# First unit's q issued from ScalarE's queue, second unit's transposed q and k copied out in two parts, in a fused attention and two-layer kernel

## The chip, the cores and the metric

The kernel runs on one core of a Trainium2 chip. The metric is the device time of one execution in microseconds (us); of several runs the median is taken. The text calls the engines by the names of the profile: PE (matrix multiply) with its weight load PEld, DVE (vector), ACT (scalar, which also computes exp), POOL and SP. SP, ACT and POOL each have an instruction queue from which they issue DMA transfers; the rows of those issues carry the names SPq, ACTq and POOLq.

## The reference

Attention over 8 batches of 12 heads, 448 positions and head size 64, followed by two matrix products with a leaky ReLU between them:

```python
scores = (1 / sqrt(64)) * q @ k^T            # per batch and head: 448 x 448
attn = exp(scores - max) / (sum + 1e-9)
x = concat_heads(attn @ v)                    # 3584 x 768
h = x @ w_in                                  # 768 -> 2048
out = maximum(0.01 * h, h) @ w_out            # 2048 -> 768, float32
```

## The kernel before

One function builds the whole program, and the order of the instructions on each engine is written out by hand (a manual schedule; later stages are ordered by a small planner with a fixed model of times, which is evaluated while the program is built and so doesn't react to the run). The work is cut into 48 units: one unit is two heads of one batch. For each unit the kernel

1. loads q, k and v from HBM (`load_one`, line 170, as float32 on a given queue; `load_soft`, line 153, on POOL's queue with a cast to bfloat16 on the way);
2. rearranges or casts them to bfloat16 (`cast`, line 183: DVE for the first units, POOL later; for unit 0 the helper `both`, line 263, gives one head to ACT and the other to DVE);
3. turns q and k so that the head dimension lies on the partitions. For the first units PE does this (`transposes`, line 294): four transposes of 112 columns each for q and four for k, written into a PSUM bank and copied to the tile `qkT` (line 305). The two PSUM banks `g0` and `g1` are handed out alternately by `next_bank` (line 74);
4. computes score blocks: `scores(u, c)` (line 311), two matrix products per block, four blocks per unit, into three PSUM slots `sc` that go round;
5. applies exp on ACT to each block (`expo`, line 326; its operations have lines 331 and 334);
6. multiplies with v on PE (`pv`, line 365, whose products have line 362) and normalises on DVE (lines 374 and 375). The result is turned and becomes the input of `x @ w_in`.

The six units of the first batch are written out by `first(u)`. From unit 6 on, attention is interleaved with the matrix products of the two layers, which make up most of the program (lines 424, 548, 645, 682).

The start, around which the change lies, runs in this order. Lines 217 to 219 issue three loads on SP's queue: k of unit 0, q of unit 0, k of unit 1. Lines 222 to 229 issue, on POOL's queue, q of unit 1, q and k of units 2 and 3, v of unit 0 and so on. They all go to parts of the tile `w_in_mix`, and later to `w_mix`, which aren't needed for their own purpose yet. PE runs seven matrix products on a zeroed tile (`warm_up`, line 241). ACT loads its function table and makes a one-element copy (line 237). Then come the casts of unit 0, k first and then q, on ACT (line 264) and DVE (line 265) together.

`transposes(0)` is already in two parts, k and then q. After each part's four transposes stand five more products on the zeroed tile (`stay_warm`, line 247). k's part is copied out by ACT, q's part by DVE. `cast(1)` follows on DVE, q and then k. `first(0)` puts on PE the first three score blocks of unit 0, one more zeroed product, the eight transposes of unit 1 into one bank, and the fourth score block; DVE copies unit 1's turned q and k out of that bank in one operation of 128 x 896. `first(1)` continues with the scores of unit 1, which need both halves of that copy.

ACT, DVE and PE each work strictly in the order of the program. An instruction that waits holds up everything behind it on its engine.

Of the kernel before, what the change touches and what calls it, by code (L numbers as in the profile page):

```python
# [16 lines left out]
def kernel(  # L17
# [9 lines left out]
    nc = tc.nc  # L27
# [118 lines left out]
    def room(x, new):  # L146

        n = P if x and new else SC
        if not rooms:
            return ld_pool.tile([n, 2, NSC, D], F32, name="f" + "qkv"[x])  # L150
        return rooms.pop(0)[:n].bitcast(F32).rearrange("p (h so d) -> p h so d", h=2, so=NSC)
# [18 lines left out]
    def load_one(u, x, queue):  # L170
        b, hp = divmod(u, HP)
        t = room(x, False)
        queue.dma_start(
            out=t.rearrange("p h so d -> p h (so d)"),
            in_=(q, k, v)[x][b, 2 * hp:2 * hp + 2].rearrange("h (p so) d -> p h (so d)", so=NSC),
        )
        raw.setdefault(u, {})[x] = t
# [37 lines left out]
                nc.gpsimd.dma_start(out=o, in_=i)  # L215

    load_one(0, 1, nc.sync)
    load_one(0, 0, nc.sync)
    load_one(1, 1, nc.sync)
    ident = const_pool.tile([P, P], BF16)  # L220
    make_identity(nc, ident)
# [21 lines left out]
    def stay_warm(n):  # L243

        ps = next_slot()
        for _ in range(n):
            nc.tensor.matmul(ps[:, 0, :P], warm[:, :P], warm[:, :P], start=True, stop=True)
# [42 lines left out]
    def turn_tile(bank):  # L290
        bank = next_bank() if bank is None else bank
        return bank.bitcast(BF16)

    def transposes(u, bank=None):
        n = SC if u < HY else P
        t, flat = qkb[u % NB], qkT[u % NQ].rearrange("p i c s -> p (i c s)")[:, :2 * NSC * n]
        for parts in ((1,), (0,)) if u == 0 else ((0, 1),):
            tr = turn_tile(bank)[:, :2 * NSC * n].rearrange("p (i s) -> p i s", i=2)
            for i in parts:
                for so in range(NSC):  # L300
                    nc.tensor.transpose(tr[:, i, ts(so, n)], t[:n, i, so].rearrange("p h d -> p (h d)"), ident[:n, :n])  # L301
            if u == 0:
                stay_warm(5)
            at = slice(parts[0], parts[-1] + 1)
            (nc.scalar.copy if u == 0 and parts == (1,) else nc.vector.tensor_copy)(
                flat.rearrange("p (i s) -> p i s", i=2)[:, at], tr[:, at]
            )
# [301 lines left out]
    kept, parts = {}, []  # L609
# [257 lines left out]
    def first(u):  # L867
# [11 lines left out]
        if u == 1:  # L879
            transposes(u + 1)  # L880
# [5 lines left out]
        if u != 1:  # L886
            transposes(u + 1)
# [13 lines left out]


    transposes(0)
    cast(1, (0, 1), fast)
    for u in range(HP):
# [344 lines left out]
```

## Time and profile before

| what | value |
|---|---|
| median of three runs (lowest, highest) | 378.0 us (377.62, 378.05) |
| the profiled execution's own time | 377.8 us |
| its span in the profile | 376.0 us |
| busy: PE, DVE, ACT, POOL | 368.8, 255.9, 259.9, 190.6 us |
| first exp (ACT, line 331) starts | 6.36 us |
| DMA: bytes moved, mean rate | 48.08 MB, 128 GB/s |

The profile counts from the start of the span; the 1.8 us between the span and the execution's time lie outside it. A row of the timeline has the start, the duration, the engine, the line, the operation with its output and input tiles, and in brackets the time that the engine was idle before it and what ended that idle time. A row of DMA issues has the tiles, the queue, the number of issues, the size of each and the time from issue to landing. A row by windows has, for each stretch, the busy time and the number of instructions of each engine, the granted PE clock, the busy share of the 16 DMA engines and the rate.

### The profile page before, as it was taken

The numbers are of one execution on the slowest core, as the hardware profiler recorded it, in microseconds if no ns is written. First come the engines' busy times: TensorE is split into PE (matmuls) and PEld (weight loads), VectorE is DVE, ScalarE is ACT, GpSimd is POOL, SyncE is SP. The second block draws the span as 40 slices with busy tenths as digits, with TensorE's granted clock in tenths as the row PEclk, the third lists the DMA queues.
The fourth block names the chain that finished last, engine by engine and source line by source line (L and its number), as shares of the span: only waits on it lengthen the run. The fifth ranks groups of instructions, "written<-read, shape, count | busy, mean of one in ns | idle before, by whom it ended". The sixth has DMA issues, their size and how long they took to land.

```text
span 376.0 us, 10120 instructions
## 1 busy us (share of the span) xinstructions
PE 368.8 (98%) x4008; PEld 265.3 (71%) x4008; DVE 255.9 (68%) x559; ACT 259.9 (69%) x399; POOL 190.6 (51%) x376
## 2 busy tenths in 40 slices
PE   7999999999999999999999999999999999999996
PEld 3665658756698566996569966699665995679765
DVE  4764868767666967676686665875747775685763
ACT  6998895866768785758766587666787668636721
POOL 8985871996269979634588335692346020000000
PEclk9999999999999999999999999999999999999999
DMA  9999999999499876963969648999445740321123
GB/s 155 200 203 207 175 203 202 166 165 168 92 186 150 113 149 89 204 154 55 162 120 150 138 65 80 166 145 180 63 66 108 131 110 0 80 57 45 41 65 105
DMA packets 99600, 48.08 MB, mean 128 GB/s; under 512 B 64608, under 2 KB 96352, under 8 KB 99552
## 3 DMA queue, kind: packets, MB, share of 16 engines
q0 software_dynamic: 39600, 22.47, 45.6%
q1 hardware_dynamic: 59504, 24.50, 32.5%
q8 instruction: 31, 0.51, 0.6%
q10 hardware_dynamic: 448, 0.47, 0.4%
q14 instruction: 17, 0.14, 0.1%
HBM read 45.61 MB, written 11.01 MB: 151 GB/s over the span
## 4 chain that ended last, share of the span: by engine, by line
PE 95%; DMA 2%; DVE 1%; POOL 1%; ACT 1%; issue 0%; POOLq 0%; ACTq 0%
PE g L682 30%; PE g L548 14%; PE sc L548 14%; PE sc L322 7%; PE sc L350 6%; PE g L424 4%; PE sc L319 4%; PE sc L645 4%; PE sc L362 3%; PE g L820 2%; PE sc L343 2%; DMA w_in_mix<-in_v_dram 2%; PE g L362 1%; PE g L301 1%; PE sc L424 1%; POOL w_in_mix L163 1%
## 5 line engine op out<-in xcount | busy, mean ns | idle before, releaser
L331 ACT ACTIVATE e<-sc 128x896 bf16<-128x896 f32 (+1 forms) x144 | 123.6, 921 | 29.9 <-PE sc L322 20.4
L682 PE MATMUL g<-w_out_sb,h 128*128 128x384 bf16 (+1 forms) x440 | 84.1, 325 | 0.0
L682 PEld LDWEIGHTS <-h 128*128 128x128 bf16 x592 | 54.4, 98 | 41.2 <-issue 11.0
L537 ACT ACTIVATE h<-c 128x512 bf16<-128x512 f32 (+1 forms) x72 | 43.1, 610 | 30.2 <-DVE c L563 12.4
L548 PEld LDWEIGHTS <-w_in_sb 128*128 128x128 bf16 x576 | 54.6, 98 | 5.7
L190 POOL COPY qkb<-fq 112x512 bf16<-112x512 bf16 x34 | 22.6, 666 | 43.8 <-DMA qkT<-qkb 34.7
L548 PEld LDWEIGHTS <-w_in_mix 128*128 128x128 bf16 x432 | 40.5, 98 | 3.7
L201 POOL COPY v<-fv 128x384 bf16<-128x384 bf16 x30 | 17.7, 591 | 42.7 <-PE sc L350 40.2
L687 DVE COPY o<-g 128x384 f32<-128x384 f32 x47 | 26.0, 553 | 13.2 <-PE g L682 13.0
L350 PE MATMUL sc<-v,e 128*128 128x65 bf16 x720 | 33.3, 193 | 0.0
L322 PE MATMUL sc<-qkT 64*128 64x448 bf16 (+1 forms) x210 | 32.8, 352 | 0.0
L978 DVE RECIPROCAL rec<-sc 112x8 f32<-112x8 f32 x42 | 8.7, 207 | 34.7 <-PE sc L350 19.4
L350 PEld LDWEIGHTS <-e 128*128 128x128 bf16 x720 | 31.1, 98 | 1.3
L979 DVE TENSOR_TENSOR x<-sc,rec 112x512 bf16<-112x512 f32 x42 | 29.0, 691 | 1.6 <-DVE rec L978 0.2
L548 PE MATMUL g<-xT,w_in_sb 128*128 128x256 bf16 (+1 forms) x216 | 28.5, 268 | 0.0
L548 PE MATMUL sc<-xT,w_in_sb 128*128 128x256 bf16 (+1 forms) x216 | 28.5, 268 | 0.0
L693 DVE TENSOR_TENSOR o<-o,g 128x384 f32<-128x384 f32 x39 | 21.4, 550 | 9.0 <-PE g L682 4.4
L343 PE MATMUL sc<-v,e 128*128 128x130 bf16 x120 | 26.5, 221 | 0.0
L649 DVE TENSOR_TENSOR o<-o,sc 128x192 f32<-128x192 f32 x39 | 13.7, 351 | 18.3 <-PE sc L645 18.3
L682 PE MATMUL g<-w_mix,h 128*128 128x384 bf16 x128 | 24.6, 326 | 0.0
L163 POOL DMA_DIRECT2D fv<-in_v_dram x32 | 20.1, 641 | 7.8 <-DMA fq<-in_q_dram 2.9
L682 PE MATMUL g<-w_mix,hmix 128*128 128x384 bf16 x112 | 21.7, 326 | 0.0
(149 smaller groups left out, 742.4 us busy)
## 6 DMA issues: line engine op xcount, KB each, us to landing
fq<-in_q_dram POOLq DMA_DIRECT2D x17, 224.0 KB, 6.1
w_out_sb<-in_moe_w_out_dram POOLq DMA_DIRECT2D x4, 768.0 KB, 13.2
out_dram<-o SPq DMA_DIRECT2D x7, 336.0 KB, 3.3
w_in_sb<-in_moe_w_in_dram POOLq DMA_DIRECT2D x2, 1152.0 KB, 13.6
out_dram<-o SPq DMA_DIRECT2D x7, 288.0 KB, 3.1
fk<-in_k_dram POOLq DMA_DIRECT2D x15, 128.0 KB, 6.0
fv<-in_v_dram POOLq DMA_DIRECT2D x15, 128.0 KB, 5.1
out_dram<-o SPq DMA_DIRECT2D x7, 240.0 KB, 3.1
```

What stands on the lines that cost most here:

```text
L163: nc.gpsimd.dma_start(out=t[p, :n, :, :so].rearrange("p u h so d -> p (u h) (so d)"), in_=(q, k, v)[x][b, hs, keys].rearrange("h (p so) d ...
L190: by(t[:SC, x].rearrange("p so h d -> p h so d"), f)
L322: nc.tensor.matmul(ps[:, j, :S].rearrange("p (so s) -> p so s", so=NSC), t[p, 1, c], t[p, 0, :, :SC], start=True, stop=True,)
L331: nc.scalar.activation(e[:, :, c, :], ps[:n, :, :S], AX.Exp, scale=scale)
L343: nc.tensor.matmul(ps, e[:, EM + qc * SC:EM + qc * SC + P], vt[:, 2 * KC:].rearrange("p j d -> p (j d)"), start=True, stop=False, skip_gro ...
L350: nc.tensor.matmul(ps[:, j * (D + 1):(j + 1) * (D + 1)], e[:, at:at + P], vt[:, j * KC + c], start=False, stop=(c == KC - 1), skip_group_c ...
L537: nc.scalar.activation(hs[:, m:m + 2, cols], x.rearrange("p (m t) -> p m t", m=2), AX.Prelu, alpha=0.01)
L548: nc.tensor.matmul(ps[:, j * nh:(j + 1) * nh], w[:, kk, ts(j, P)], x[:, kk], start=(first and j == 0 and kk == 0), stop=(kk == KH - 1), sk ...
L682: nc.tensor.matmul(ps[:, cols], x[:, m], w[:, m], start=(first and m == 0), stop=(m == MH - 1), skip_group_check=True,)
L687: by(o[:, at], ps[:, :NW])
L693: nc.vector.tensor_add(o[:, at], o[:, at], ps[:, :NW])
L979: nc.vector.tensor_mul(x, ps[:, :, :, :D], rec.to_broadcast([SC, 2, 2 * NP, D]))
```

## The change

```diff
     load_one(0, 1, nc.sync)
-    load_one(0, 0, nc.sync)
+    load_one(0, 0, nc.scalar)
     load_one(1, 1, nc.sync)
...
-        for parts in ((1,), (0,)) if u == 0 else ((0, 1),):
+        for parts in ((1,), (0,)) if u == 0 else ((0,), (1,)) if u == 1 else ((0, 1),):
```

The load of unit 0's q becomes the first instruction of ACT, ahead of the load of its function table. SP keeps the loads of k of unit 0 and k of unit 1, which now follow each other directly. No other queue's order changes.

For unit 1, the loop over `parts` in `transposes` runs twice, q first and then k. Each turn takes a bank of its own, so q's four transposes go to `g0` and k's four to `g1`, and each is followed by a DVE copy of 128 x 448, in place of one of 128 x 896. The five zeroed products after each part belong to unit 0 alone and aren't added. Because one more bank is handed out, `g0` and `g1` change places in everything that follows; the order of the instructions, their sizes and their neighbours in the alternation stay the same.

## The prediction

> **What bounds the kernel now.** I read the page's busy shares and its chain of waits first, then ACT by form over the first 26 us, the windows after that, and last the timeline and the DMA issues of the first 11 us, where the change lies.
>
> ```profile
> PE 368.8 (98%) x4008; PEld 265.3 (71%) x4008; DVE 255.9 (68%) x559; ACT 259.9 (69%) x399; POOL 190.6 (51%) x376
> ...
> PE 95%; DMA 2%; DVE 1%; POOL 1%; ACT 1%; issue 0%; POOLq 0%; ACTq 0%
> ```
>
> Over the whole span PE is the bound. The change touches no PE work of the later stages, so the question is when PE's unbroken stretch begins. ACT over the first 26 us, by form:
>
> ```profile
> L331 ACT ACTIVATE e<-sc 112x896 bf16<-112x896 f32 x18 | 15.3, 943 | 0.9 <-PE sc L319 0.9
> L334 ACT ACTIVATE c<-sc 112x896 bf16<-112x896 f32 x6 | 5.8, 959 | 0.0
> ```
>
> These are the 24 exp operations of the first six units. The idle time before all of them together is 0.9 us, and it lies before the first. From there on ACT is never idle until this row of its timeline, where PE takes over:
>
> ```profile
> 26.08 1.73 ACT L331 ACTIVATE e<-sc 112x896 bf16<-112x896 f32 x2 [0.16 <-PE sc L319]
> ```
>
> PE by windows at that point (PE's busy time is the second number after the colon):
>
> ```profile
> 18.00:24.00 6.00, 5.59 (x101) 3.72 (x99) 4.26 (x12) 6.00 (x8) 4.63 (x8) 1.00 1.43 198
> 24.00:30.00 6.00, 6.00 (x90) 3.88 (x89) 3.18 (x11) 4.56 (x6) 6.00 (x11) 1.00 1.18 210
> 30.00:36.00 6.00, 6.00 (x42) 2.74 (x40) 3.33 (x5) 5.22 (x9) 3.84 (x5) 1.00 1.19 209
> ```
>
> Up to about 24 us ACT is full (6.00 of 6.00) and PE is not; after it PE is full. So the end of the kernel is set by the start of the first exp, then by 24 exps without a gap, then by PE. A first exp that starts later by some time makes the end later by all of it. One that starts earlier pays only while scores are ready: the chain of waits has this where ACT and PE meet.
>
> ```profile
> 20.75 0.17 issue
> 20.92 0.97 ACT e L331
> ```
>
> The scores of that exp were ready 0.17 us before ACT took them, so a gain beyond about 0.2 us would meet PE there, which itself hangs on v of unit 0 (below).
>
> What sets the first exp: the ACT timeline, and the DMA issues of the first two loads (time to landing last).
>
> ```profile
> 3.79 0.40 ACT L264 CAST qkb<-w_in_mix 112x256 bf16<-112x256 f32 x1 [1.56 <-DMA w_in_mix<-in_k_dram]
> 4.65 0.40 ACT L264 CAST qkb<-w_in_mix 112x256 bf16<-112x256 f32 x1 [0.45 <-DMA w_in_mix<-in_q_dram]
> 4.96 0.53 ACT L305 COPY qkT<-g 128x448 bf16<-128x448 bf16 x1
> ...
> 6.36 0.92 ACT L331 ACTIVATE e<-sc 112x896 bf16<-112x896 f32 x1 [0.87 <-PE sc L319]
> ```
>
> ```profile
> 0.75 0.40 SPq L173 DMA_DIRECT2D w_in_mix<-in_k_dram  x1
> 1.20 0.45 SPq L173 DMA_DIRECT2D w_in_mix<-in_q_dram  x1
> ```
>
> ```profile
> w_in_mix<-in_k_dram SPq DMA_DIRECT2D x1, 224.0 KB, 3.0
> ...
> w_in_mix<-in_q_dram SPq DMA_DIRECT2D x1, 224.0 KB, 3.4
> ```
>
> k lands at 0.75 + 3.0 = 3.75, q at 1.20 + 3.4 = 4.60. Now PE between them:
>
> ```profile
> 4.25 0.32 PEld L301 LDWEIGHTS <-qkb 112*128 112x128 bf16 x4 [0.79 <-ACT qkb L264]
> 4.51 0.53 PEld L247 LDWEIGHTS <-hmix 128*128 128x128 bf16 x5
> 5.10 0.21 PEld L301 LDWEIGHTS <-qkb 112*128 112x128 bf16 x4
> 5.27 0.32 PEld L247 LDWEIGHTS <-hmix 128*128 128x128 bf16 x5
> 5.51 0.39 DVE L305 COPY qkT<-g 128x448 bf16<-128x448 bf16 x1 [0.63 <-PE g L301]
> ```
>
> k's four transposes and the five zeroed products behind them keep PE from 4.25 to 4.51 + 0.53 = 5.04. q's transposes start at 5.10, which is 0.05 after q's cast ended on ACT (4.65 + 0.40 = 5.05). This is the key to the change: q's load is late by no more than 0.06 us, because PE is occupied with k's part until 5.04 anyway. After that q is copied at 5.51, and the first exp starts at 6.36, that is 6.36 - 5.10 = 1.26 later than q's transposes.
>
> **The change part by part.** *q of unit 0 on ACT's queue.* The load leaves SP's second place, so it can be issued 1.20 - 0.75 = 0.45 us earlier. ACT pays one issue of about 0.45 us (the SP row) ahead of this one:
>
> ```profile
> 0.74 1.28 ACT L237 ACT_TABLE_LOAD   x1 [0.74 <-PEq L1234]
> ```
>
> The table would end at about 0.74 + 0.45 + 1.28 = 2.47 and the small copy behind it 0.2 later. ACT then still has over 1 us until 3.79, so this costs nothing; without that cover it would cost 0.45. SP's last early load, k of unit 1, moves up by about 0.45.
>
> What matters is k of unit 0, on which PE's order hangs. It no longer has the DMA engines for itself. The windows (last two columns: DMA share, GB/s):
>
> ```profile
> 1.50:2.00 0.50, 0.50 (x2) 0.15 (x1) 0.42 (x1) 0.50 (x1) 0.47 (x1) 1.00 0.25 72
> 2.00:2.50 0.50, 0.50 (x3) 0.20 (x2) 0.33 (x2) 0.22 (x2) 0.50 (x2) 1.00 0.67 215
> 2.50:3.00 0.50, 0.50 (x3) 0.23 (x2) 0.47 (x2) 0.00 (x0) 0.50 (x1) 1.00 0.90 295
> 3.00:3.50 0.50, 0.50 (x3) 0.18 (x2) 0.21 (x4) 0.00 (x0) 0.50 (x2) 1.00 1.07 313
> ```
>
> A load is 224 KB, 229 thousand bytes. The first two windows carry 36 + 107 thousand and the next ones 295 to 313 GB/s, so k's bytes are through at about 2.5 + 86/295 = 2.79, and both loads' 459 thousand at about 3.55. Each lands about 1.0 us after that. There was room up to 2.5 us (share 0.25 and 0.67), then none. Bounds for k's landing: 3.75 if q only fills the room, and 4.60 if the two take turns and nothing goes faster than now. Below 3.75 I exclude it, since k already had no company. My value: both queues together run at the full 304 GB/s from about 1.7 on, so 459/304 = 1.5 us, to 3.2, and both land at about 4.2. That is k later by 0.45, q earlier by 0.4.
>
> The Trainium skill, "DMA: Bandwidth & Descriptors", section "Issuing engines are not separate DMA queues", speaks against this edit: transfers from different issuing engines run on the same 16 DMA engines and interleave, and only the issuing time is saved. By that rule alone the two loads would end together near q's old time, k late by about 0.85; the share of 0.25 and 0.67 in the windows says that there is some room, and no run here shows two such loads side by side yet.
>
> With k at 4.20: casts at 4.24, q's cast on ACT right behind (the next ACT operation followed q's cast after 4.96 - 4.65 = 0.31), ended by 4.95. k's transposes start at 4.25 + 0.45 = 4.70. The nine weight loads took 0.79 at their pace of then; the second five took 0.32 in place of 0.53, so PE's pace had changed by about 5.05. Four loads at the old pace and five at the new: 4.70 + 0.35 + 0.32 = about 5.40 in place of 5.10. So **+0.30 us**. At the ends: k at 3.75 gives 5.04, -0.06; k at 4.60 gives 5.10 + 9 x 0.064 = 5.68, +0.58, or 5.10 + 0.79 = 5.89, +0.79, at the old pace.
>
> *Unit 1's copy in two parts.*
>
> ```profile
> 7.40 0.29 DVE L190 COPY qkb<-w_in_mix 112x512 bf16<-112x512 bf16 x1 [1.49 <-DMA w_in_mix<-in_q_dram]
> 7.61 0.42 DVE L190 CAST qkb<-w_in_mix 112x512 bf16<-112x512 f32 x1
> 8.49 0.62 DVE L305 COPY qkT<-g 128x896 bf16<-128x896 bf16 x1 [0.47 <-PE g L301]
> ```
>
> Now DVE idles 0.47 us and copies all at 8.49 to 9.11. After: q's half goes into that idle time (8.07 to 8.46, 0.39 by the 128x448 row above), k's half follows at 8.49 and ends at 8.88, 0.23 earlier. DVE works 2 x 0.39 - 0.62 = 0.16 more, inside its idle time; it is free 0.23 earlier for the casts of unit 2. Should k's transposes finish early, there's no loss either; if the cover of 0.47 were gone, it would cost 0.16. The second bank adds no wait, since its last use was long before. Scores then start at 8.95 in place of 9.18 (first row below is PE's). But ACT can't use it:
>
> ```profile
> 9.18 0.36 PE L319 MATMUL sc<-qkT 64*128 64x448 bf16 x2 [0.43 <-DVE qkT L305]
> ```
>
> ```profile
> 8.79 0.92 ACT L334 ACTIVATE c<-sc 112x896 bf16<-112x896 f32 x1
> 9.61 0.91 ACT L331 ACTIVATE e<-sc 112x896 bf16<-112x896 f32 x1
> ```
>
> Unit 1's first exp follows after 0.82, and the spacing between unit 0's exps is about 0.81 (6.36 to 8.79 is three of them). So at most 0.02 us is to be had now, and with unit 0 later by 0.30 nothing: this part is a reserve of about 0.25 + 0.3 us against a late q or k of unit 1. Those land late because of the queues, at 1.53 + 5.8 = 7.33 for q:
>
> ```profile
> w_in_mix<-in_q_dram POOLq DMA_DIRECT2D x1, 112.0 KB, 5.8
> ```
>
> I take no change there, since the bytes ahead of it are the same. v of unit 0 holds the next gate on DVE, and a later ACT gives it more slack, not less:
>
> ```profile
> 10.22 0.48 DVE L198 COPY x_mix<-w_in_mix 112x512 bf16<-112x512 bf16 x1 [0.31 <-DMA w_in_mix<-in_v_dram]
> ```
>
> **Sum.** +0.30 and 0.00: 377.8 + 0.3 = 378.1 against the profiled execution, which lies 0.2 below the median; against the median, 378.0 + 0.3 = 378.3 us. This is under 0.2% (0.76 us), about what a measurement of this kernel can tell from no change.
>
> **The rivals.** *k is not slowed* (k lands up to 3.85). For it: the room in the first two windows. Against it: the share of 0.90 to 1.07 from 2.5 on, when k still has 86 thousand bytes to come. PE's zeroed products cap the gain at 0.06, the copy adds 0.02: 377.9, from 377.8 to 378.1. *The edit doesn't do what it says*: the two queues are fed in turn, and nothing lands earlier than q did. k at 4.60: +0.58 to +0.79, so 378.6 to 378.8; it straddles the bound of 0.2%.
>
> *Slower, through PE's pace.* PE's warm-up products end at 4.37 (1.20 + 3.17 by this row), where k's transposes now follow without a gap:
>
> ```profile
> 1.20 3.17 PE L241 MATMUL g<-hmix 128*128 128x512 bf16 x7 [1.20 <-DVE gate L236]
> ...
> 7.75 0.70 PE L301 MATMUL g<-ident,qkb 112*128 112x112 bf16 x8 [0.72 <-DVE qkb L190]
> ```
>
> With k at 4.20 a gap of about 0.3 opens on PE, at 4.60 one of 0.7, right before the pace changes at about 5.05. If that gap puts the change off until after unit 1, then k's nine loads keep the slow pace (+0.79 in the late case), q's four transposes and the first scores take about 0.2 each longer (q's four loads 0.21 against 0.32 for k's, likewise the products behind), together about +1.2: 379.2. It decides once the gap is a sizeable part of the time over which the pace is set. For it: the pace did change at that place. Against it: the idle 0.72 us of PE after 7 us didn't bring the slow pace back. The Trainium skill, "TensorE: Matmul & The Clock Gate", Part 1, tells of a clock that doubles after about 3.4 us of sustained work in a free-running window; the trace fits with a change near 5.05 after a start at 1.20, and no run here shows what a gap does.
>
> **How the numbers follow.** Forecast, k late by 0.2 to 0.6: 0.47. k not slowed: 0.23. Both at q's old time: 0.12, of which half is beyond 0.2%. Slow pace or an unseen later landing of unit 1's loads: 0.12. Faster by over 0.2%, for which no row gives a mechanism: 0.06. So slower 0.06 + 0.12 = 0.18, faster 0.06, same 0.76. The range takes the ends of k's landing (-0.1 to +0.8 on 378.0) and 0.2 for the spread of the runs, rounded: 377.6 to 379.0.
>
> **What would show it.** In the changed profile: the landing of k of unit 0 (forecast 4.2), PE's weight loads at lines 301 and 247 (4.70 and 5.40), the first exp at about 6.66, ACT without a gap after it, DVE's second half copy well ahead of unit 1's first exp, and PE full from about 24 us. Wrong would be: a k that lands at 3.8, a gap on ACT between unit 0 and unit 1, or a first exp whose shift doesn't reach the end.

## The result and the profile after

Over 22 runs each, the changed kernel has a median of 378.85 us (377.77 to 381.03) and the kernel before one of 377.97 us (377.44 to 379.29). The ratio is 1.0021, with a 95% interval of 1.0011 to 1.0030: the change costs 0.8 us by the ratio and 0.88 us by the medians, at the edge of 0.2%. It lies inside the range of the prediction (377.6 to 379.0), above its 378.3. The profiled execution of the changed kernel took 379.23 us, which is above its median; its span is 377.5 us.

The page still shows PE as the bound; the chain of waits now holds more of ACT.

```profile
PE 369.7 (98%) x4008; PEld 266.0 (70%) x4008; DVE 257.2 (68%) x560; ACT 259.9 (69%) x399; POOL 192.0 (51%) x376
...
PE 91%; ACT 4%; DVE 2%; issue 1%; DMA 1%; ACTq 0%
```

First come the loads. These are the rows of the timeline in which the loads are issued:

```profile
0.74 0.43 ACTq L173 DMA_DIRECT2D w_in_mix<-in_q_dram  x1
...
0.75 0.90 SPq L173 DMA_DIRECT2D w_in_mix<-in_k_dram  x2
...
1.20 1.28 ACT L237 ACT_TABLE_LOAD   x1 [1.20 <-PEq L1234]
```

These are the same loads in the view of DMA issues, with the time to landing last:

```profile
w_in_mix<-in_q_dram ACTq DMA_DIRECT2D x1, 224.0 KB, 4.0
w_in_mix<-in_k_dram SPq DMA_DIRECT2D x1, 224.0 KB, 3.6
```

q is issued 0.46 us earlier and lands at 0.74 + 4.0 = 4.74, which is later than the 4.60 of before. k lands at about 4.35 in place of 3.75. Both loads lost. The windows say where (DMA share and GB/s last):

```profile
1.50:2.00 0.50, 0.50 (x2) 0.15 (x1) 0.42 (x1) 0.50 (x1) 0.48 (x1) 1.00 0.39 78
2.00:2.50 0.50, 0.50 (x3) 0.20 (x2) 0.33 (x2) 0.49 (x2) 0.50 (x2) 1.00 0.90 141
2.50:3.00 0.50, 0.50 (x3) 0.23 (x2) 0.46 (x2) 0.19 (x1) 0.50 (x1) 1.00 0.91 279
3.00:3.50 0.50, 0.50 (x3) 0.18 (x2) 0.21 (x4) 0.00 (x0) 0.50 (x2) 1.00 1.08 379
```

From 2.0 to 2.5 us the DMA engines moved less than before (141 GB/s against 215). Here they were also busier (0.90 against 0.67), but that isn't part of the pattern: in a second profile of the same kernel they were less busy and moved less still:

```profile
2.00:2.50 0.50, 0.50 (x3) 0.20 (x2) 0.33 (x2) 0.49 (x2) 0.50 (x2) 1.00 0.32 33
```

The room that the prediction saw there was not used.

Then ACT, in its timeline:

```profile
4.33 0.86 ACT L264 CAST qkb<-w_in_mix 112x256 bf16<-112x256 f32 x2 [1.64 <-DMA w_in_mix<-in_k_dram]
5.38 0.53 ACT L305 COPY qkT<-g 128x448 bf16<-128x448 bf16 x1 [0.18 <-PE g L301]
7.25 0.92 ACT L331 ACTIVATE e<-sc 112x896 bf16<-112x896 f32 x1 [1.34 <-PE sc L319]
```

and PE's weight loads:

```profile
4.78 0.32 PEld L301 LDWEIGHTS <-qkb 112*128 112x128 bf16 x4 [1.33 <-ACT qkb L264]
5.04 0.56 PEld L247 LDWEIGHTS <-hmix 128*128 128x128 bf16 x5
5.56 0.44 PEld L301 LDWEIGHTS <-qkb 112*128 112x128 bf16 x4
5.95 0.35 PEld L247 LDWEIGHTS <-hmix 128*128 128x128 bf16 x3
```

k's transposes start 0.53 later (4.78 against 4.25) and q's 0.46 later (5.56 against 5.10). The first exp is 0.89 later (7.25 against 6.36), because PE's pace had not changed yet (in the kernel before it changed at about 5.05): from q's transposes to the first exp it took 7.25 - 5.56 = 1.69 in place of 1.26. The form view shows it in the mean of the ten weight loads of zeroed products, 147 ns, where those five of before that stand behind q's transposes have 97:

```profile
L247 PEld LDWEIGHTS <-hmix 128*128 128x128 bf16 x10 | 1.1, 147 | 0.0
L301 PEld LDWEIGHTS <-qkb 112*128 112x128 bf16 x8 | 0.8, 138 | 1.3 <-ACT qkb L264 1.3
```

The column of the granted clock reads 1.00 in these early windows at either pace, so the early pace has to be read from durations.

After the first exp ACT has no gap up to the handover to PE, as before:

```profile
26.88 1.72 ACT L331 ACTIVATE e<-sc 112x896 bf16<-112x896 f32 x2 [0.17 <-PE sc L319]
```

That is 0.80 after the same exp of before (26.08). The rest of this execution's difference in span (377.5 - 376.0 = 1.5) comes later. One DVE operation that combines weights took 2.21 us, PE waited for the DVE operation behind it, and that wait is in PE's windows (2.74 of 3.00; PE was full there before):

```profile
41.83 2.21 DVE L473 TENSOR_TENSOR w_in_mix<-w_in_sb,w_in_mix 128x768 bf16<-128x768 bf16 x1
```

```profile
44.92 0.37 PE L319 MATMUL sc<-qkT 64*128 64x448 bf16 x2 [0.26 <-DVE x L979]
```

```profile
42.00:45.00 3.00, 2.74 (x51) 1.90 (x48) 2.97 (x4) 2.06 (x4) 3.00 (x6) 1.00 1.43 166
```

Why that operation took so long wasn't settled. The padded kernel below, whose loads are those of before, has the same late start and a comparable loss, so this operation isn't needed to explain the median.

### The profile page after: what moved, and what is told of

It is laid out like the page before. It is cut to its first block, busy times and chain, and to the rows that moved or that the text cites. A ratio compares the mean times of both kernels' runs of the same rounds, so it can differ in the third digit from the quotient of the medians.

```text
span 377.5 us, 10121 instructions
## 1 busy us (share of the span) xinstructions
PE 369.7 (98%) x4008; PEld 266.0 (70%) x4008; DVE 257.2 (68%) x560; ACT 259.9 (69%) x399; POOL 192.0 (51%) x376
## 4 chain that ended last, share of the span: by engine, by line
PE 91%; ACT 4%; DVE 2%; issue 1%; DMA 1%; ACTq 0%
PE g L682 30%; PE g L548 14%; PE sc L548 14%; PE sc L322 7%; PE sc L350 6%; PE sc L645 4%; ACT e L331 3%; PE sc L319 3%; PE sc L362 3%; PE g L424 2%; PE g L820 2%; PE sc L343 2%; DMA w_in_mix<-in_k_dram 1%; PE g L362 1%; PE g L301 1%
## 5 line engine op out<-in xcount | busy, mean ns | idle before, releaser
L190 POOL COPY qkb<-fq 112x512 bf16<-112x512 bf16 x34 | 25.1, 739 | 43.3 <-DMA qkT<-qkb 34.2
L319 PE MATMUL sc<-qkT 64*128 64x448 bf16 x144 | 20.1, 356 | 2.3 <-ACT e L331 1.5
```

Of the source, the lines that this page charges most:

```text
L190: by(t[:SC, x].rearrange("p so h d -> p h so d"), f)
L319: nc.tensor.matmul(ps[:, j, :S], t[p, S + c * SC:S + c * SC + P], t[p, :S], start=True, stop=True)
```

## The experiments

Theory A, formed after the result: q beside k makes k of unit 0 late, PE and ACT start late by that much or more, and all of it reaches the end; the split copy pays nothing. Rivals: B, the split copy carries part of the loss; C, k of unit 1, now right behind k of unit 0 on SP's queue, is the cause; D, the gap that opens on PE puts off its change of pace. Each kernel was timed against the kernel before on the same chip, with 22 runs of the changed kernel's first timing and 5 (k of unit 1 behind q) to 12 of the others. One profile was taken of each, so that landings and first exps are single values, while the times are medians; with the loads as before, k landed at 3.75, 3.55 and 3.75. The ratio isn't the quotient of the two medians, and differs from it by up to 0.08%.

| kernel | k of unit 0 lands | first exp | median against before | ratio, 95% interval |
|---|---|---|---|---|
| before | 3.75 | 6.36 | | |
| changed | 4.35 | 7.25 | 378.85 / 377.97 | 1.0021 (1.0011 to 1.0030) |
| issue only | 4.65 | 7.89 | 378.96 / 378.13 | 1.0034 (1.0012 to 1.0057) |
| split only | 3.55 | 6.40 | 377.93 / 378.13 | 0.9994 (0.9985 to 1.0002) |
| k of unit 1 behind q | 4.85 | 7.88 | 379.56 / 378.13 | 1.0032 (1.0020 to 1.0044) |
| eight warm-ups | 4.45 | 7.00 | 378.51 / 378.13 | 1.0012 (1.0003 to 1.0021) |
| halves | 3.45 and 3.64 | 6.39 | 377.80 / 377.97 | 0.9997 (0.9988 to 1.0007) |
| q later | 3.7 | 7.68 | 378.82 / 377.97 | 1.0015 (1.0003 to 1.0026) |
| padded before | 3.75 | 7.42 | 379.02 / 377.97 | 1.0027 (1.0018 to 1.0036) |
| changed again | 4.65 | 7.08 | 378.87 / 378.01 | 1.0015 (1.0002 to 1.0029) |
| eight warm-ups again | 4.75 | 7.23 | 379.10 / 378.01 | 1.0022 (1.0012 to 1.0032) |
| halves, short | 3.25 and 3.44 | 6.11 | 377.74 / 378.01 | 0.9992 (0.9983 to 1.0001) |
| halves side by side | 3.45 and 4.1 | 7.16 | 378.11 / 377.99 | 1.0009 (0.9994 to 1.0023) |
| k beside k | 4.35 | 7.67 | 379.24 / 377.99 | 1.0032 (1.0020 to 1.0044) |

The landings are the time of issue plus the time to landing of the DMA view; "q later" and the second half of "halves side by side" are read from the casts that waited for them.

### Each part alone

Issue only, against the kernel before:

```diff
-    load_one(0, 0, nc.sync)
+    load_one(0, 0, nc.scalar)
```

> Part 1 alone: q of unit 0 on ACT's queue, unit 1's copy left in one piece. Theory A (q takes turns with k, the late k does all the damage): k of unit 0 lands at about 4.3 and q at about 4.7 as in the changed kernel, first exp at about 7.2, time within 0.3 us of the changed kernel (378.6 to 379.1). Rival B (the split copy, with its change of banks and its extra DVE operation, carries part of the loss): first exp as late, but the time back at 378.0 to 378.4.

Measured: 0.83 us over before. DMA view of this kernel:

```profile
w_in_mix<-in_q_dram ACTq DMA_DIRECT2D x1, 224.0 KB, 4.2
w_in_mix<-in_k_dram SPq DMA_DIRECT2D x1, 224.0 KB, 3.9
```

k lands at 4.65 and q at 4.94. The first part alone has the whole loss of the change. The profiled execution is the slowest of the twelve (383.11 against a median of 378.96), so it is read here only up to the first exp, which came at 7.89 and not at the 7.2 expected; what happened to it later is said below.

Split only, against the kernel before:

```diff
-        for parts in ((1,), (0,)) if u == 0 else ((0, 1),):
+        for parts in ((1,), (0,)) if u == 0 else ((0,), (1,)) if u == 1 else ((0, 1),):
```

> Part 2 alone: both loads on SP's queue, unit 1's copy in two pieces. Theory A: unit 1's scores start about 0.2 earlier than 9.18, unit 1's first exp at 9.59 to 9.61 as before, time 377.8 to 378.1, no change. Rival B: 378.4 or more.

Measured: 0.20 us under before, with an interval that includes no change; a gain of up to 0.15% isn't excluded, a loss beyond 0.02% is. Its timeline shows unit 1's first exp where it was before (9.61), although the two copies end at 8.55 in place of 9.11. In this profile unit 1's casts also started earlier than before (6.80 against 7.40), so the end of the copies isn't the split's doing alone:

```profile
7.75 0.80 DVE L305 COPY qkT<-g 128x448 bf16<-128x448 bf16 x2
```

```profile
9.60 0.94 ACT L331 ACTIVATE e<-sc 112x896 bf16<-112x896 f32 x1
```

Rival B fell: the split costs nothing, and ACT takes the scores when it is free.

### What makes k late

The edits from here on are against the changed kernel, unless another is named.

```diff
-    load_one(1, 1, nc.sync)
+    load_one(1, 1, nc.scalar)
```

> The changed kernel with k of unit 1 issued behind q on ACT's queue, so that SP has k of unit 0 alone. Theory A (k and q of unit 0 share packet by packet): k of unit 0 unchanged at about 4.3, q no longer shares with k of unit 1 once k of unit 0 is through and lands at about 4.4 in place of 4.74; first exp about 0.1 earlier at most, since PE is held by k's part; time 378.5 to 379.0. Rival C (the early k of unit 1, close behind on SP's queue, is what makes k of unit 0 late): k of unit 0 back at about 3.8, first exp at 6.4, time 378.0.

Measured: 1.43 us over before. DMA view:

```profile
w_in_mix<-in_q_dram ACTq DMA_DIRECT2D x1, 224.0 KB, 4.4
w_in_mix<-in_k_dram SPq DMA_DIRECT2D x1, 224.0 KB, 4.1
```

With nothing behind it on SP's queue, k of unit 0 landed at 4.85, later than in the changed kernel. That speaks against rival C, though k of unit 1 was still issued at 1.20, on the other queue; the next kernel decides it. Theory A's details fell too: q was expected at 4.4 and landed at 5.14, the first exp was expected up to 0.1 earlier and came 0.63 later (7.88), and the time is above the 378.5 to 379.0 expected.

In the next kernel q's load stands behind the function table and the small copy in ACT's order:

```diff
-    load_one(0, 0, nc.scalar)
+    q0_t = room(0, False)
...
     nc.scalar.copy(gate[:, :1], gate[:, 1:])
+    nc.scalar.dma_start(
+        out=q0_t.rearrange("p h so d -> p h (so d)"),
+        in_=q[0, 0:2].rearrange("h (p so) d -> p h (so d)", so=NSC),
+    )
...
```

> The changed kernel with q of unit 0 issued by ACT only after its function table and the small copy, at about 2.3. Theory A: k of unit 0 has no company from q until its bytes are nearly through and lands at 3.75 to 3.85; q lands at about 5.5 or later, and now q sets the first exp, at 7.2 to 7.8; time 378.7 to 379.5. Rival C (k of unit 1 close behind is the cause): k of unit 0 stays at about 4.3.

Measured: 0.85 us over before. The load didn't wait for the table: it was issued at 1.20, beside it, and not at the 2.3 expected. So the strict order on ACT, which the description of the kernel before states, doesn't hold for the issue of this DMA. It comes 0.46 after k in place of level with it, and k is back at 3.7, as its cast shows (timeline):

```profile
1.20 0.40 ACTq L238 DMA_DIRECT2D w_in_mix<-in_q_dram  x1
```

```profile
3.74 0.40 ACT L269 CAST qkb<-w_in_mix 112x256 bf16<-112x256 f32 x1 [1.52 <-DMA w_in_mix<-in_k_dram]
5.38 0.41 ACT L269 CAST qkb<-w_in_mix 112x256 bf16<-112x256 f32 x1 [1.24 <-DMA w_in_mix<-in_q_dram]
```

k of unit 1 stands directly behind k of unit 0 on SP's queue here, as in the changed kernel, and k of unit 0 isn't late: rival C fell. q now sets the start. It was issued at the moment of before and landed 0.7 later (5.3 against 4.60). That fits with k of unit 1, which was issued at the same moment on the other queue and can have shared with it, but wasn't tested. So a second queue helps neither load here.

Now both loads are cut by head. SP and ACT each issue one head of k and then one head of q (`load_half` is `load_one` for one head):

```diff
-    load_one(0, 1, nc.sync)
-    load_one(0, 0, nc.scalar)
...
+    for x in (1, 0):
+        t = room(x, False)
+        for j, queue in enumerate((nc.scalar, nc.sync)):
+            load_half(0, x, t, j, queue)
```

> The changed kernel with both loads of unit 0 cut by head: each of the queues of SP and ACT issues one head of k and then one head of q, so that two queues feed k alone first. Theory A (k is late because q takes turns with it, and there was room for more packets before 2.5 us): k lands at 3.5 to 3.75, q at 4.3 to 4.6, first exp at 6.2 to 6.4, time 377.7 to 378.0. Against it: if two queues slow each other whatever they carry, k lands at 4.0 or later and the first exp comes after 6.6.

Measured: 0.17 us under before, with an interval that includes no change. k's heads, in the DMA view, and the rate in the window:

```profile
w_in_mix<-in_k_dram ACTq DMA_DIRECT2D x1, 112.0 KB, 2.9
w_in_mix<-in_k_dram SPq DMA_DIRECT2D x1, 112.0 KB, 2.7
```

```profile
2.00:2.50 0.50, 0.50 (x3) 0.19 (x2) 0.33 (x2) 0.50 (x1) 0.50 (x2) 1.00 0.83 234
```

k lands at 3.64 at the latest although two queues are busy. So it isn't the second queue as such that hurts, but what it carries beside k.

Two more kernels ask about the low rate of the first microsecond. The first, against the kernel with halves, has k's two heads on SP's queue and q's two on ACT's; the second has k of unit 1 on ACT's queue and q of unit 0 back in SP's second place:

```diff
-    for x in (1, 0):
+    for x, queue in ((1, nc.sync), (0, nc.scalar)):
         t = room(x, False)
-        for j, queue in enumerate((nc.scalar, nc.sync)):
+        for j in range(2):
             load_half(0, x, t, j, queue)
```

```diff
-    load_one(0, 0, nc.scalar)
-    load_one(1, 1, nc.sync)
+    load_one(0, 0, nc.sync)
+    load_one(1, 1, nc.scalar)
```

> Loads of unit 0 cut by head as in the kernel with halves, but k's two halves on SP's queue and q's two on ACT's, so that q runs beside k as in the changed kernel. If q beside k is what slows the first microsecond, the rate from 2.0 to 2.5 us is 33 to 141 GB/s as in the runs with q beside k, k's second half lands at 4.3 or later, first exp at 7.0 or later, time 378.6 to 379.2. If it is the size of the load (two whole loads being issued at once), the rate is 170 to 235, k lands by about 4.1, first exp at 6.6 to 6.9, time 378.1 to 378.5.

> The changed kernel with k of unit 1 on ACT's queue in place of q of unit 0, which goes back to SP's second place: two whole loads side by side, both of k. If any whole load beside k slows it, the rate from 2.0 to 2.5 us is 33 to 141 GB/s, k of unit 0 lands at 4.3 or later and q at 5.0 or later, first exp at 7.2 or later, time 378.8 to 379.5. If only q beside k does, the rate is 170 or more and k of unit 0 lands at 3.8 to 4.1; q then lands at about 4.8, first exp at 6.6 to 6.9.

Measured: 0.12 us over before (the interval includes no change) and 1.25 us over. The windows of the two kernels, in this order:

```profile
2.00:2.50 0.50, 0.50 (x3) 0.20 (x2) 0.33 (x2) 0.50 (x1) 0.50 (x2) 1.00 0.68 219
```

```profile
2.00:2.50 0.50, 0.50 (x3) 0.20 (x2) 0.33 (x2) 0.49 (x1) 0.50 (x2) 1.00 0.74 186
```

Neither has the low rate, yet k beside k lands at 4.35, as in the changed kernel, and its q at 1.20 + 4.2 = 5.4. So in this profile sharing alone made k of unit 0 late by 0.6: the low rate isn't needed for that. Halves side by side met the expectation for the size of the load in rate, landing and time, but its first exp came at 7.16 and not by 6.9, since PE's five zeroed loads behind q's transposes still took 0.56 us at 5.79, the slow pace. The low rate was seen in the profiles with a whole load of q beside a whole load of k (141, 66, 82, 37, 33 and 94 GB/s in the changed kernel, issue only, k of unit 1 behind q, eight warm-ups, changed again and eight warm-ups again), and in neither of these two. Why stays open.

### Whether the gap on PE matters

```diff
-    warm_up(7)
+    warm_up(8)
```

> The changed kernel with eight warm-up products in place of seven, so that PE has no gap between 4.37 and 4.79. Rival D (the gap puts off PE's change of pace, which costs about 0.3 of the 0.89 us by which the first exp is late): weight loads fall from 0.15 to 0.10 at about 5.1 again, first exp at about 6.9, time 0.3 us under the changed kernel. If the pace goes by a window that doesn't mind the gap, the loads stay at 0.15 up to about 7 in some executions, and first exp and time are those of the changed kernel (378.85).

Measured: 0.38 us over before, and in the profile a gap of only 0.14 us, the zeroed loads at a mean of 122 ns and the first exp at 7.00. That spoke for rival D. So it was run again beside the changed kernel itself:

> The changed kernel itself, a second profile and times beside the two below. Theory A: k of unit 0 lands at 4.2 to 4.6 again, first exp at 7.0 to 7.6, time 378.6 to 379.0. If k lands at 3.8 this time, the landing in the first profile was one draw and theory A loses its ground.

> The changed kernel with eight warm-up products, now beside the changed kernel on the same chip. Rival D (the gap puts off PE's change of pace): weight loads fall to 0.10 before 6 us again, and the time is 0.3 to 0.4 us under the changed kernel's. If the moment of the change is a draw that doesn't mind the gap (the padded kernel had no gap and changed at about 6.5): times within 0.2 us of each other over the rounds.

Measured on one chip: changed 378.87, eight warm-ups 379.10 (before 378.01). The expected gain of 0.3 to 0.4 didn't come. But in the profile of eight warm-ups again k landed at 4.75 and a gap of 0.59 us was left behind the eighth product, so the gap wasn't taken away. The weight loads of the changed kernel, second profile:

```profile
5.33 0.23 PEld L301 LDWEIGHTS <-qkb 112*128 112x128 bf16 x4 [1.87 <-ACT qkb L264]
5.51 0.32 PEld L247 LDWEIGHTS <-hmix 128*128 128x128 bf16 x5
5.78 0.25 PEld L301 LDWEIGHTS <-qkb 112*128 112x128 bf16 x4
```

```profile
7.08 2.53 ACT L331 ACTIVATE e<-sc 112x896 bf16<-112x896 f32 x3 [0.79 <-PE sc L319]
```

Here the gap was about 1 us (1.06 in PE's row at 5.36), and yet PE ran at the quick pace from the first load behind it (0.32 for five). This doesn't refute rival D, because the pace had changed before the gap: the last of the seven warm-up products took 0.57 in place of the 0.63 of before (first row here, then before):

```profile
3.73 0.57 PE L241 MATMUL g<-hmix 128*128 128x512 bf16 x1
```

```profile
3.73 0.63 PE L241 MATMUL g<-hmix 128*128 128x512 bf16 x1
```

The other half of the answer is the kernel before with more zeroed products behind k's transposes, which has no gap:

```diff
-                stay_warm(5)
+                stay_warm(13 if parts == (1,) else 5)
```

> The kernel before, with loads untouched, and thirteen in place of five zeroed products behind k's transposes of unit 0: the first exp is put off by PE work alone, by about 8 x 0.064 to 8 x 0.107 = 0.5 to 0.85 us. Theory A (every part of a us by which the first exp is late comes out at the end): time 378.5 to 378.8. Rival: later stages absorb it, 378.0 to 378.2. More than 0.85 above before would mean that the shift meets something worse downstream.

```profile
4.48 1.42 PEld L247 LDWEIGHTS <-hmix 128*128 128x128 bf16 x13
5.85 0.44 PEld L301 LDWEIGHTS <-qkb 112*128 112x128 bf16 x4
6.24 0.51 PEld L247 LDWEIGHTS <-hmix 128*128 128x128 bf16 x5
```

Here PE had no gap, and its pace was still the slow one at 6.24. So the moment of the change differs between executions without any gap. That kernel's first exp is 1.06 later and its median 1.05 us longer, with loads untouched (more than the 0.85 expected, since q's transposes and the five products behind them ran at the slow pace too). A late first exp came out at the end in full.

What wide gaps do is seen in the single zeroed product behind unit 0's first scores (issue only, k beside k, before):

```profile
8.53 0.61 PE L241 MATMUL g<-hmix 128*128 128x512 bf16 x1
```

```profile
8.31 0.61 PE L241 MATMUL g<-hmix 128*128 128x512 bf16 x1
```

```profile
6.63 0.39 PE L241 MATMUL g<-hmix 128*128 128x512 bf16 x1
```

PE was still at the slow pace past 8.3 us in issue only, k of unit 1 behind q, q later and k beside k, whose gaps before k's transposes (in q later, before q's) were 1.01, 1.00, 0.78 and 0.49. In the six profiles with a gap of at most 0.14 it had changed by 6.7. With 0.29 and 0.42 (halves side by side, changed) it changed at about 7, with 0.59 (eight warm-ups again) at about 5.7. So rival D didn't fall: wide gaps go with a late change in most of these profiles. No kernel opened a gap with the loads untouched, so it isn't shown either.

There is also a second loss, which the first profile of the changed kernel doesn't show. In its second profile PE's granted clock fell to half from about 11 to 14 us, and ACT then waited for scores:

```profile
11.00:14.00 3.00, 3.00 (x43) 2.43 (x42) 1.26 (x4) 2.75 (x4) 3.00 (x6) 0.50 1.43 197
```

```profile
14.46 2.53 ACT L331 ACTIVATE e<-sc 112x896 bf16<-112x896 f32 x3 [0.56 <-PE sc L319]
```

Its first exp was 0.72 late, and the exp of the handover 1.59 (27.67 against 26.08). The profile of issue only has such a drop from 14 to 17 us and its handover is 3.86 late, the larger part of that execution's excess in span (381.3 - 376.0 = 5.3). A mean granted clock of 0.996 or less, as these two executions have, is on record for 7 of the 22 executions of the changed kernel and for 3 of the 11 timed again, but for 3 of 99 of the kernel before in the experiments and for none of 43 of the padded kernel, split only and the two kernels that load k by halves on both queues; the other kernels have 15 of 68. The changed kernel's executions with it have medians of 379.19 and 379.36, those without it 378.46 and 378.43, that is 0.4 to 0.5 over before. So about half of the 0.9 goes with such drops. In both profiles the drop followed a stretch in which PE had little to do (busy 0.56 of the microsecond from 10, and 0.03 of that from 12); what sets it off wasn't tested.

In the other profiles with a first exp late by over 0.6, the handover is late by about as much, for example 1.44 of 1.52 (k of unit 1 behind q), 1.34 of 1.32 (q later), 0.98 of 1.06 (padded), 0.72 of 0.80 (halves side by side). The last kernel's median is nevertheless only 0.12 over before, so the first exp of one profile doesn't stand for all executions.

### A version that starts sooner

This is the kernel with halves, with one zeroed product in place of five behind k's transposes:

```diff
-                stay_warm(5)
+                stay_warm(1 if parts == (1,) else 5)
```

> The kernel with the loads cut by head, with one in place of five zeroed products behind k's transposes of unit 0. The claim is that those products, and not q, hold q's transposes: q's transposes start right after q's cast, at about 4.8 in place of 5.07; first exp at 6.0 to 6.2; time 377.5 to 377.8, the fastest version so far but hardly to be told from it. Against it: PE's pace changes later with fewer products, and the first exp comes at 6.4 or later.

```profile
6.11 2.53 ACT L341 ACTIVATE e<-sc 112x896 bf16<-112x896 f32 x3 [0.80 <-PE sc L329]
```

Measured: 377.74 against 378.01. The first exp is the earliest of all, 0.25 before that of the kernel before, which agrees with the claim that the zeroed products held q's transposes. The interval (0.9983 to 1.0001) just includes no change, so this is no proven gain.

## Why the prediction was right, and where its sizes were off

*What bounds the kernel.* Right in the main. The first exp sets the end: the padded kernel (first exp +1.06, time +1.05) shows it with the loads untouched. That the shift of the changed kernel, +0.89, and its median, +0.88, agree is in part luck: about half of the median goes with drops of PE's clock, which the prediction didn't have, and in such an execution its sign "ACT without a gap" failed (0.56 at 14.46). The value of +0.30 was too small by a factor of about three; the time lies inside the range because the range took in k at 4.60 and 0.2 for the spread.

*q on ACT's queue.* The direction and the place were right: k is slowed by q's company, and PE's order hangs on k. The term was mis-sized: k was put later by 0.45 and was later by 0.6 and 0.9. The prediction let both queues fill the room before 2.5 us, run at the full 304 GB/s and land together at 4.2, with q earlier by 0.4. Measured in two profiles of the changed kernel: k at 4.35 and 4.65, q at 4.74 and 5.04. The upper bound of 4.60 for k was no bound; the low rate from 2.0 to 2.5 us wasn't in it. The Trainium skill, "DMA: Bandwidth & Descriptors", section "Issuing engines are not separate DMA queues", says that transfers of several issuers interleave and that only issuing time is saved. By that rule k would land near 4.60 and q unchanged, as the prediction worked out; the traces agree for k and are worse for q (k 4.35 to 4.85, q 4.74 to 5.14 in the kernels with q level with k). It should have had more weight than the room in the windows.

*From k to the first exp.* The prediction put +0.45 for k down to +0.30, because PE's pace would change at 5.05 as in the kernel before. That moment isn't fixed: the padded kernel was still slow at 6.24, and the second profile of the changed kernel was quick before 4.3. At the slow pace the step from q's transposes to the first exp took 1.69 in place of the 1.26 assumed; at the quick pace it took 7.08 - 5.78 = 1.30 in the second profile. So k later by 0.6 at the slow pace made the first exp 0.89 late, and k later by 0.9 at the quick pace made it 0.72 late.

*The split copy.* Right: nothing to be had while ACT is full (0.9994, 0.9985 to 1.0002). Unit 1's loads, which it was held in reserve for, even came earlier in the changed kernel (q of unit 1 in 4.4 us in place of 5.8).

*The rivals.* "k is not slowed" fell with the landings. "Nothing lands earlier than q did" (378.6 to 378.8) is in substance what happened, with a chance of 0.12, and should have been the forecast. "Slower, through PE's pace" named a cost that is there: in the four kernels with a slow pace past 8.3, six score products of unit 0 took 1.30 us in place of 0.74. Whether the gap is the trigger stays open. The Trainium skill, "TensorE: Matmul & The Clock Gate", Part 1, calls the window free-running; the profiles agree, in that the same kernel changed pace after 6.3 in one execution and before 4.3 in the other.

*Left open.* Why whole loads of q and k side by side start at 33 to 141 GB/s; whether a gap puts off PE's change of pace, and what halves its clock later in some executions; why the DVE operation at 41.83 took 2.21 us; whether the split and the halves together gain 0.1%.

## What to carry to other kernels

Loads that are needed in order stood best on one queue in that order here: a second queue for the second load made the first one late, and the chain that hangs on the first paid for it. Giving the second queue a part of the first load did no harm, and its gain isn't proven. Before pulling a transfer forward, look at whether its consumer was waiting at all: here it was late by 0.06 us. And look at the granted clock of every execution, not of the profiled one alone: a median can mix two losses.

## What wasn't expected

In q later, ACT issued a DMA that stood behind its function table and a small copy in program order at 1.20, while the table was still loading (0.74 to 2.02). And two whole loads of q and k side by side moved 33 to 141 GB/s from 2.0 to 2.5 us, where one queue alone moved 170 to 215 (before, padded, split only) and one head of k on each of two queues 193 and 234.
